# Output projections of a segment recurrence: rows stationary in four column tiles, weights moving, the last eight rows of four segments in one more pass

## The chip, the cores and the metric

One core of one Trainium2 chip runs the whole program. The metric is the device time of one execution in microseconds (us). Each kernel was run several times, in rounds that alternate with runs of the kernel before on the same chip. Most executions of one kernel agree within about 0.3%. Where stages are compared, each number is read from one profiled execution; profiles of two kernels can come from different chips of the same machine, so a stage difference of under about 15 us in the forward or backward stage is not used alone.

In the views PE is TensorE (PEld its weight loads), DVE VectorE, ACT ScalarE, POOL GpSimd and SP SyncE; L201 is a line of the kernel, x24 a count. A pair is a weight load and its matmul. The granted clock is the share of TensorE's full clock that was granted; the DMA share is the mean busy share of the core's 16 DMA engines.

## The reference, cut to what matters

A layer normalisation, a recurrent attention block A and a gated MLP block B, forward, and the gradients of all inputs. Block A works through 64 segments of 32 rows. Eight memory rows go ahead of each segment, so a segment has L = 40 rows, and the first eight rows of its output are the memory of the next one:

```python
for s in range(n_seg):                                  # 64, one after the other
    h = concatenate([mem, x[:, s*32:(s+1)*32, :]])      # 40 rows of 512
    q, k, v = (einsum('btd,dhe->bhte', h, W) for W in (Wq, Wk, Wv))   # 32 heads of 128
    ...                                                 # masked softmax, o = p v
    o = einsum('bhte,hed->btd', o, Wo)                  # output projection: 40 x 4096 by 4096 x 512
    mem = o[:, :8, :]                                   # to the next segment
    outs.append(o[:, 8:, :])
```

The backward pass goes through the segments in reverse. It has three such projections per segment, of dV, dK and dQ, summed into one 40 x 512 result; its first eight rows go to the segment before. The change touches these four projections and what is done with their results.

## The kernel before

A helper layer orders the instructions: it takes the program in source order, estimates readiness, and fixes an order for each engine. The output projection keeps a 128 x 128 block of the weight stationary and moves the 40 rows of a segment (as columns); the result is transposed, 128 features by 4 x 40:

```python
def outproj(pi):                                  # forward; before
    heads = range(pi * PG * 3, min(H, (pi + 1) * PG * 3))
    for c in range(DC):                           # 4 blocks of 128 features
        for h in heads:                           # 32 heads in three calls
            g_, hl = h // 3, h % 3
            nc.tensor.matmul(at_ps[0][:, c, :], lhsT=Wo[:, h, c * 128:(c + 1) * 128],
                             rhs=OT[:, g_ * GW + hl * L:g_ * GW + (hl + 1) * L], ...)
...
nc.scalar.activation(hT_next[:, :, 0:M], at_ps[0][:, :, 0:M], AF.Copy)   # memory of the next segment
nc.vector.tensor_copy(aoT[:], at_ps[0][:, :, M:L])
nc.gpsimd.dma_start(self.AOT[s], aoT[:])          # 32 rows, transposed, for the middle stage
```

The backward one, `dht`, is the same three times. The middle stage (MLP, in tiles of 128 rows) needs the rows upright, so it transposes them:

```python
# middle stage, tile j; before (cut)
nc.gpsimd.tensor_copy(aoC[:]..., aoT[:])          # GpSimd reorders
for c in range(DC):
    nc.tensor.transpose(tp[:, c, :], st["aoC"][:, c * 128:(c + 1) * 128], self.ident[:])
nc.scalar.activation(a_rows[:], tp[...], AF.Copy)  # ScalarE evicts
nc.vector.tensor_tensor(t0[:], a_rows[:], ga_bc[:], op=ALU.mult)
nc.vector.tensor_tensor(x1[:], t0[:], st["x0"][:], op=ALU.add)
```

The last stage (weight gradients in 44 groups of up to three heads, one 2 MB load `xt` each, issued by SyncE and GpSimd in turn, plus 16 layernorm tiles spread between the groups) does the same with the row gradients: four loads, four transposes, a VectorE copy and a GpSimd cast per tile. Its two side matrices take their memory rows by two transposed loads, `mt`, and transposes.

The softmax here doesn't subtract the row's maximum and nothing guards it: scores larger than these inputs give would overflow.

## Time and profile before

Before: 4352.75 us, median of four runs (4343.44 to 4357.68). The stages are cut at the first projection, the last forward projection, the first and last product of the backward segments, and the end; the lengths are read from the view that sums busy time by windows.

| stage (us) | before, first profile | before, second profile |
|---|---|---|
| forward segments | 1378.7 | 1394.5 |
| middle (MLP) | 695.6 | 697.3 |
| backward segments | 1306.9 | 1317.3 |
| last (weight gradients) | 847.7 | 846.8 |
| span | 4315.0 | 4342.0 |

### The profile page before, as it was taken

What the parts mean: (1) busy time and instruction counts of PE and PEld (TensorE: products, weight loads), DVE (VectorE), ACT (ScalarE), POOL (GpSimd) and SP (SyncE); (2) the same over time, 40 slices, a digit from 0 to 9 for tenths busy, and PEclk for the clock granted to TensorE, in tenths of its full rate; (3) what the DMA queues carried; (4) which work ended last, traced back from release to release, by engine and by line L of the source; (5) the groups of instructions that cost most, each with busy time, mean ns of one, the idle gap of its engine ahead of it and who ended that gap; (6) DMA issues with size and microseconds to landing.
All of it is one profiled execution on the core that took longest, in us unless ns stands there. A gap on an engine that the chain in (4) does not pass through costs nothing. (4 is left out here: it accounts for less than half of the span.)

```text
span 4315.0 us, 189475 instructions
## 1 busy us (share of the span) xinstructions
PE 3762.5 (87%) x87970; PEld 3165.2 (73%) x87970; DVE 1964.5 (46%) x3832; ACT 1537.9 (36%) x2685; POOL 807.3 (19%) x1063
## 2 busy tenths in 40 slices
PE   2989999999999688887988989898899949999996
PEld 2888888888888644444588889898888836666653
DVE  3444444444444377761233433343343346566554
ACT  0333333333343344441222222222222236556553
POOL 2111111111111133321111111111111112222210
PEclk6999999999999899998999999999999969999998
DMA  6223322233222422227754455455455498777873
GB/s 223 95 95 106 101 101 101 101 103 105 100 103 101 157 99 99 97 80 245 210 192 153 154 162 174 154 169 164 156 156 173 142 176 164 161 163 160 163 154 111
DMA packets 597548, 606.56 MB, mean 141 GB/s; under 512 B 404026, under 2 KB 492362, under 8 KB 595092
## 3 DMA queue, kind: packets, MB, share of 16 engines
q1 hardware_dynamic: 526756, 316.52, 28.2%
q0 software_dynamic: 64272, 264.56, 18.4%
q8 instruction: 687, 11.26, 1.1%
q10 hardware_dynamic: 5728, 13.37, 0.9%
q14 instruction: 105, 0.86, 0.1%
HBM read 319.30 MB, written 275.02 MB: 138 GB/s over the span
## 5 line engine op out<-in xcount | busy, mean ns | idle before, releaser
L1217 PE MATMUL gps<-rows,hrows 128*128 128x384 bf16 (+1 forms) x2640 | 461.9, 322 | 3.8 <-ACT ot L61 2.5
L1217 PEld LDWEIGHTS <-hrows 128*128 128x128 bf16 x2640 | 252.8, 98 | 139.0 <-issue 5.7
L63 DVE COPY rows<-tpg 128x384 bf16<-128x384 bf16 (+1 forms) x616 | 195.8, 347 | 265.5 <-PE tpg L1210 161.0
L1080 DVE CAST dh1T<-dh_ps 128x128 bf16<-128x128 f32 x64 | 18.7, 292 | 588.9 <-ACT dyT L1069 588.9
L1034 PE MATMUL dh_ps<-dQT,WqT 128*128 128x40 bf16 x8192 | 234.6, 182 | 55.1 <-issue 54.8
L347 PE MATMUL proj_ps<-hT,Wq 128*128 128x40 bf16 x8192 | 240.2, 180 | 34.0 <-issue 17.5
L1034 PEld LDWEIGHTS <-WqT 128*128 128x128 bf16 x8192 | 223.1, 98 | 61.1 <-issue 60.9
L1034 PE MATMUL dh_ps<-dKT,WkT 128*128 128x40 bf16 x8192 | 233.1, 179 | 37.8 <-issue 37.3
L347 PE MATMUL proj_ps<-hT,Wk 128*128 128x40 bf16 x8192 | 241.3, 180 | 22.7 <-issue 22.2
L347 PEld LDWEIGHTS <-Wq 128*128 128x128 bf16 x8192 | 229.1, 96 | 42.0 <-issue 41.5
L984 PE MATMUL proj_ps<-dyT,WoT 128*128 128x40 bf16 x8192 | 233.4, 181 | 23.0 <-ACT dyT L1069 18.0
L1034 PEld LDWEIGHTS <-WkT 128*128 128x128 bf16 x8192 | 222.1, 96 | 41.8 <-issue 41.3
L984 PEld LDWEIGHTS <-WoT 128*128 128x128 bf16 x8192 | 227.9, 97 | 30.2 <-issue 29.8
L1034 PE MATMUL dh_ps<-dVT,WvT 128*128 128x40 bf16 x8192 | 239.9, 179 | 9.0 <-issue 8.8
L347 PEld LDWEIGHTS <-Wk 128*128 128x128 bf16 x8192 | 227.0, 96 | 25.2 <-issue 25.1
L1203 ACT ACTIVATE xr<-xt 128x3072 bf16<-128x3072 bf16 (+1 forms) x44 | 235.3, 5349 | 11.2 <-DMA dhT<-DH1T 6.1
L347 PE MATMUL proj_ps<-hT,Wv 128*128 128x40 bf16 x8192 | 236.1, 180 | 2.7 <-issue 2.2
L1210 PEld LDWEIGHTS <-xr 128*128 128x128 bf16 x2560 | 180.3, 98 | 77.8 <-issue 28.4
L1034 PEld LDWEIGHTS <-WvT 128*128 128x128 bf16 x8192 | 227.3, 96 | 11.4 <-issue 11.2
L1210 PE MATMUL tpg<-ident,xr 128*128 128x128 bf16 x2560 | 218.1, 220 | 17.5 <-DVE rows L63 5.9
L347 PEld LDWEIGHTS <-Wv 128*128 128x128 bf16 x8192 | 226.4, 96 | 4.1 <-issue 3.9
L429 PE MATMUL at_ps<-OT,Wo 128*128 128x40 bf16 x8192 | 226.0, 179 | 0.0
(308 smaller groups left out, 7638.4 us busy)
## 6 DMA issues: line engine op xcount, KB each, us to landing
VT<-VT POOLq DMA_DIRECT2D x64, 384.0 KB, 2.7
OT<-OT POOLq DMA_DIRECT2D x64, 384.0 KB, 3.5
PS<-Pst POOLq DMA_DIRECT2D x64, 384.0 KB, 3.1
QST<-Qst POOLq DMA_DIRECT2D x64, 384.0 KB, 3.2
KST<-Kst POOLq DMA_DIRECT2D x64, 384.0 KB, 4.7
OT_l<-OT SPq DMA_DIRECT2D x64, 384.0 KB
VT_l<-VT SPq DMA_DIRECT2D x64, 384.0 KB
Pst_l<-PS SPq DMA_DIRECT2D x64, 384.0 KB
```

Source lines behind the costliest of these rows:

```text
L63: return nc.vector.tensor_copy(out, in_)
L347: nc.tensor.matmul(ps[:, g_, hl * L:(hl + 1) * L], lhsT=Ws[w][:, c, h * E:(h + 1) * E], rhs=hT[:, c, :], start=(c == 0), stop=(c == DC - 1))
L429: nc.tensor.matmul(at_ps[0][:, c, :], lhsT=Wo[:, h, c * 128:(c + 1) * 128], rhs=OT[:, g_ * GW + hl * L:g_ * GW + (hl + 1) * L], start=(n_a ...
L984: nc.tensor.matmul(ps[:, g_, hl * L:(hl + 1) * L], lhsT=WoT[:, c, h * E:(h + 1) * E], rhs=dyT[:, c, :], start=(c == 0), stop=(c == DC - 1))
L1034: nc.tensor.matmul(dh_ps[0][:, c, :], lhsT=WT[:, h, c * 128:(c + 1) * 128], rhs=X[:, g_ * GW + hl * L:g_ * GW + (hl + 1) * L], start=(n_dh ...
L1080: nc.vector.tensor_copy(dh1T[:], dh_ps[0][:, :, M:L])
L1203: nc.scalar.activation(xr[:, 0:cut, :], xt[:, :, 0:cut].rearrange("p s x -> p x s"), AF.Copy)
L1210: nc.tensor.transpose(ps[0:KR, hl, :], xr[:, c0:c0 + 2, :].rearrange("p a s -> p (a s)"), self.ident[:, :])
L1217: nc.tensor.matmul(ps[:, 0:nh * E], lhsT=hrows[0:KR, tp_, c * 128:(c + 1) * 128], rhs=rows[0:KR, tp_, 0:nh * E], start=(tp_ == 0), stop=(t ...
```

## The change

The intent: with 32 of the rows stationary and 128 weight columns moving, a product uses 32 of the 128 columns of the array, so four products for the four feature blocks run side by side. The eight rows that don't fit are collected for four segments (again 32 rows) and sent in one more pass. Results come out upright, as rows; only the memory rows need a transpose.

```diff
+    def col_mms(self, ps, lhsT, w, start, stop):
+        for c in range(self.cfg.DC):
+            self.nc.tensor.matmul(ps[32 * c:32 * c + 32, :], lhsT=lhsT, rhs=w[:, c * 128:(c + 1) * 128],
+                                  start=start, stop=stop, tile_position=(0, 32 * c))
...
-                    for c in range(DC):
-                        for h in heads:   # Wo stationary, 40 columns move
+                    for h in range(pi * PG * 3, min(H, (pi + 1) * PG * 3)):
+                        off = (h // 3) * GW + (h % 3) * L
+                        self.col_mms(at_ps[0], OT[:, off:off + 32], Wo[:, h, :], n_at[0] == 0, n_at[0] == H - 1)
...
-                    nc.scalar.activation(hT_next[:, :, 0:M], at_ps[0][:, :, 0:M], AF.Copy)
+                at_sb = sb2.tile([128, 128], BF16, name="at_sb")
+                nc.scalar.activation(at_sb[:], at_ps[0][:], AF.Copy)
+                tail.collect(s % nseg_t, [OT])          # GpSimd: rows 32..39 of this segment
+                tail.chunk()                            # a quarter of the pass of the last four segments
+                    self.rows_to_mem(psp, at_sb, hT_next)   # a transpose and a VectorE copy
+                tail.store_a(s, at_sb)
... (backward: the same for dV, dK, dQ)
... (middle stage)
-                nc.gpsimd.tensor_copy(aoC[:]..., aoT[:])
-                    nc.tensor.transpose(tp[:, c, :], st["aoC"][...], self.ident[:])   # x 4
-                nc.scalar.activation(a_rows[:], tp[...], AF.Copy)
+                self.load_x_rows(a_rows, j, self.AOA, self.AOB)      # eight loads per tile
... (last stage, per layernorm tile)
-                    nc.sync.dma_start(dhT[...], self.DH1T[j * nseg + s4])             # x 4
-                    nc.tensor.transpose(tp[:, c, :], dhT[:, c, :], self.ident[:])     # x 4
-                nc.vector.tensor_copy(dh[:], tp[...])
-                nc.gpsimd.tensor_copy(dhb[:], dh[:])
+                self.load_x_rows(dhb, j, self.DHA, self.DHB)         # eight loads per tile
... (side matrices: sixteen small loads of memory rows in place of two mt loads and eight groups of transposes)
```

## The prediction

> **What bounds the kernel now.** I first cut the span into its stages: forward segments (96 to 1470 us), middle (to 2150), backward segments (to 3475), weight gradients (to the end).
>
> ```profile
> core 0: us, PE busy (x) PEld busy (x) DVE busy (x) ACT busy (x) POOL busy (x), PEclk, DMA share, GB/s
> 96.00:1470.00 1374.00, 1250.37 (x39464) 1197.41 (x39463) 581.39 (x1202) 528.21 (x1158) 257.41 (x457) 0.99 0.30 101
> 2150.00:3475.00 1325.00, 1183.59 (x38180) 1155.76 (x38180) 502.82 (x1096) 310.89 (x641) 189.45 (x326) 0.97 0.51 161
> ```
>
> TensorE carries both segment stages, 21.5 and 20.7 us per segment (64 of each), with 617 and 597 matmuls per segment. The other engines are below half. The list of waits says what TensorE still waits for in the backward stage:
>
> ```profile
> PE dh_ps L1034 <- issue: 100.9, 105, 2.6
> PE proj_ps L984 <- ACT dyT L1069: 18.0, 63, 0.3
> ```
>
> "Issue" means that no operand was missing. The timeline of one such wait, beginning after 45 matmuls of a run of 128:
>
> ```profile
> 2709.64 2.17 PE L1034 MATMUL dh_ps<-dKT,WkT 128*128 128x40 bf16 x80
> 2711.65 1.28 PE L1034 MATMUL dh_ps<-dQT,WqT 128*128 128x40 bf16 x45
> 2714.82 2.26 PE L1034 MATMUL dh_ps<-dQT,WqT 128*128 128x40 bf16 x83 [1.89 <-issue]
> ```
>
> Counting matmuls from the end of that wait to the ends of the next ones:
>
> ```profile
> core 0: us, PE busy (x), PEclk, DMA share, GB/s
> 2714.80:2724.19 9.39, 8.26 (x256) 1.00 0.12 20
> 2724.20:2733.60 9.40, 7.93 (x256) 1.00 0.80 255
> 2733.60:2738.45 4.85, 4.22 (x128) 0.65 0.38 154
> 2738.45:2756.40 17.95, 15.90 (x512) 1.00 0.55 168
> ```
>
> All are multiples of 128. And the table of DMA queues has
>
> ```profile
> q8 instruction: 687, 11.26, 1.1%
> ```
>
> 687 packets of 16,384 bytes; 87,970 matmuls / 687 = 128. At 64 bytes an instruction (below), a packet is 256 instructions, 128 pairs of weight load and matmul. So TensorE's program arrives in blocks of 128 pairs, and TensorE stops where a block has not landed. I lined up the instruction packets with the block edges. Backward, a packet starts 1.05 us at the earliest (mean 1.7) after a block that had to be waited for begins, and TensorE goes on 2.2 to 2.6 us (mean 2.5) after that start. A packet started inside a block is thus the next block: only one is fetched ahead. My estimate of the time below which a block cannot go is therefore 1.7 + 2.5 = 4.2 us backward, where the data transfers take half of the DMA time; forward (0.30) about 3.7. Check: backward blocks that hold only projection matmuls last 4.3 us on average (41 blocks), although the same 128 matmuls run in 3.2 us when nothing stops them. The projections that this change speeds up are already bound by instruction delivery, not by the array.
>
> **What the Trainium skill says.** (1) "TensorE: Matmul & The Clock Gate", "Wait — 56ns, not 53.3ns?": start to start never falls below about 25 ns, however few columns move. The trace agrees: 80 matmuls of 40 columns in 2.17 us, less 0.18 for the last one's own length, is 25 ns. (2) Same page, "Part 3: Packing small matmuls", "Measured speedup vs the span model": tiles of one pack start some 4 ns apart and run together. The trace has a case, the 32-column matmuls over 384 columns in the prologue:
>
> ```profile
> 20.64 0.39 PE L190 MATMUL modrow_ps<-wmod,sclo_bc 128*32 128x384 bf16 x4
> 20.86 0.33 PE L190 MATMUL modrow_ps<-wmod,schi_bc 128*32 128x384 bf16 x4
> 21.02 0.33 PE L190 MATMUL modrow_ps<-wmod,sclo_bc 128*32 128x384 bf16 x4
> ```
>
> Four start every 0.16 us: what one alone needs for 384 columns. So column tiles do run together, and their weight loads hide. (3) "Trainium Architecture — The Big Picture", "The software stack": instructions have 64 bytes, and the streams are put into each engine's memory at load. The first agrees; the second does not, for the trace has the 687 packets during the run.
>
> **The change, part by part.**
> *Array time of the projections.* Each of the four projections (one in a forward segment, three in a backward one) was 128 pairs at 25 to 26 ns, 3.3 us. Now it is 32 heads x 4 column tiles, again 128 pairs. A group of four streams 128 columns, 53 ns plus a few (estimate: a third of the 0.16 us above): 32 x 56 ns = 1.8 us. Saved: 1.5 us forward, 4.6 backward per segment, if only the array counted.
> *Tail pass.* 128 more pairs per projection and four segments: 32 forward and 96 backward per segment, 0.45 and 1.35 us of array time. With the transpose of the memory rows the segments go to 650 and 694 matmuls. The built program has 96,124 matmuls, 8,154 more.
> *Chain from segment to segment.* Before: ACT copy of 32 columns (197 ns), TensorE idle 0.28 us. Now: ACT copy of 128 columns (estimate 0.3 us), a transpose (0.21 plus its load), a DVE copy (0.2), about 0.95 us with the handovers. The built order puts tail matmuls before the transpose in most segments, so the visible idle time is some 0.5 us, 0.2 more than before.
> *Array sum:* forward -1.5 + 0.45 + 0.2 = -0.8 us, backward -4.6 + 1.35 + 0.2 = -3.0 us per segment, together -245 us. This is the intended gain.
> *Delivery.* Backward goes from 597/128 = 4.66 blocks per segment to 694/128 = 5.42. Now a block takes 20.7/4.66 = 4.43 us. About one block per segment, the one with the dot products and the first 128-column matmuls, is bound by its own work (62 blocks of mean 4.85); the other 4.42 would all lie at the floor. With 4.1 us (4.2 less a little, as the same data is moved in more time): 4.42 x 4.1 + 4.85 = 23.0 us, +2.3 per segment, +147 us. With the floor at 3.4 it would be 19.9 us (-50); with 4.4, 24.3 (+230). Forward: unstalled segments take about 20.4 us, so 19.6 by array time. Blocks that start up to some 30 matmuls before the projection, or in its first hundred, are then shorter than 3.7 us and are stretched to it; averaged over all positions this gives back about 1 us, and late packets in the q, k, v projections (0.5 to 0.7 us per segment now) stay. 21.2 us against 21.4, and some 0.3 for more switches between tile shapes (the trace has 0.10 us at one, instead of 0.027): net about +10 us for the stage.
> *Middle stage.* 64 transposes, 16 ACT and 16 POOL copies go, 7 more loads per tile come on SP. TensorE waits there for other things (ACT duT 43 us, weights 24 us): -5.
> *Last stage.* TensorE waits 41 us for the reordered memory tiles, but the first xt lands only at 3519.9 us, which holds the start anyway. The two mt loads are 16,384 packets of 64 bytes (15 ns each over 16 engines: 15 us of saturated DMA); about 4,000 packets of 256 bytes replace them: -10. Per tile a DVE cast of 0.66 us and four transposes go, and DVE's layernorm work is in the last chain: -10. Sum -20.
> *POOL* gains the collecting copies, some 1 to 2 us per segment, off the path.
> Total: 4351 + 147 + 10 - 5 - 20 = 4483; I lean slightly to the lower side, as some packets will find quieter DMA: 4475 us.
>
> **Rivals.**
> *The array sets the pace* and delivery follows: 4351 - 245 - 25 = about 4080 us. For it: 87% busy TensorE, concurrent tiles shown. Against it: stops exactly at block edges, and pure projection blocks at 4.3 us instead of 3.2.
> *Delivery binds at its best value* (3.3 to 3.4 us per block everywhere): backward -50 to -80, forward -40, rest -25: about 4210. For it: the smallest spacing of two packets is 3.25 us. Against: the mean under DMA load is 4.2.
> *The tiles do not run together* with 128 columns, each pair still taking 25 ns: the tail pass then costs 0.8 and 2.4 us per segment also in array time. Backward hidden behind delivery; forward +60 us: about 4540. Against: the 0.16 us groups.
> *The clock falls*, since TensorE would stand idle for half of each block: one stalled window above was granted 0.65. At half clock a block of column tiles takes 3.4 us, still under the floor, but the 128-column matmuls and the dot products slow: up to 100 us more, towards 4580.
> *A bank fewer for the rotating PSUM tiles* makes TensorE wait for evictions: DVE and ACT are below half busy; a few tens of us at most.
>
> **Range and chances.** Block floors of 3.7 to 4.4 us backward (about +30 to +230), forward -50 to +60, rest -25: 4340 to 4590 for 8 times in 10. Faster by over 2% (below 4264) needs nearly the best delivery everywhere or a wrong theory: 0.09. Within 2%: 0.25. Slower by over 2% (above 4438): 0.66.
>
> **What would show it.** Right: TensorE's idle time on "issue" in the backward stage grows from some 100 to 400 us or more, its busy time falls; groups of four start about 56 ns apart between stops; about 751 instruction packets; the backward stage lasts some 1470 us, the forward one 1360 to 1400; waits fall at multiples of 128 matmuls. Wrong: a backward stage under 1300 us, blocks of column tiles below 3.3 us, or two blocks fetched ahead (the array rival); groups at 100 ns (no concurrency); a granted clock near 0.7 there (the clock rival).

## The result, and the profile after

After: 4402.91 us, median of four runs (4396.22 to 4405.3), against 4352.75: slower by 1.15%, ratio 1.0115 with a 95% interval of 1.0094 to 1.0136. The interval leaves out 1, so the loss is clear of the noise, small as it is. The forecast was +124 us and the measurement is +50.

The stages, from the view by windows; columns as in the prediction (window, length, busy time of each engine, granted clock, DMA share, GB/s). After:

```profile
86.70:1432.30 1345.60, 1243.03 (x41839) 1147.52 (x41839) 585.90 (x1235) 531.96 (x1166) 244.91 (x475) 1.00 0.30 104
1432.30:2065.70 633.40, 551.17 (x3802) 303.83 (x3790) 319.45 (x573) 230.57 (x365) 153.28 (x128) 0.95 0.50 157
2065.70:3536.00 1470.30, 1155.08 (x44351) 1034.57 (x44351) 490.79 (x1102) 315.37 (x640) 216.41 (x464) 0.92 0.44 144
3536.00:4403.50 867.50, 738.69 (x5886) 476.38 (x5874) 460.87 (x876) 447.36 (x490) 113.69 (x88) 0.94 0.72 154
```

The second profile of the kernel before:

```profile
86.10:1480.60 1394.50, 1262.07 (x39694) 1208.04 (x39692) 587.35 (x1216) 529.98 (x1160) 257.46 (x455) 0.98 0.30 100
1480.60:2177.90 697.30, 573.53 (x3866) 319.53 (x3889) 377.08 (x577) 244.19 (x386) 175.57 (x148) 0.92 0.45 144
2177.90:3495.20 1317.30, 1182.28 (x38143) 1159.83 (x38144) 500.50 (x1087) 310.27 (x639) 184.34 (x320) 0.96 0.51 160
3495.20:4342.00 846.80, 741.20 (x5957) 480.72 (x5977) 478.15 (x898) 450.86 (x495) 170.89 (x104) 0.94 0.76 158
```

Stage by stage, after less before: forward -49, middle -64, backward +153, last +21. (Against the first profile: -33, -62, +163, +20.) The backward stage holds more matmuls (44,351 against 38,143) but TensorE is busy for less of it, 1155 us against 1182, and the stage is longer.

Where TensorE stood in the backward stage after the change, from the list of waits (what waited, for what, us in all, times, longest), and the table of DMA queues:

```profile
PE dh_ps L201 <- issue: 233.2, 122, 4.5
PE dh_tps L201 <- issue: 46.8, 42, 2.0
PE proj_ps L1004 <- issue: 23.6, 28, 1.3
```

```profile
q8 instruction: 751, 12.30, 1.2%
```

"Issue", waiting for no operand, is now 304 us. All the stops on issue of this stage, counted in the trace, begin at the same count of matmuls modulo 128. 751 instruction packets for 96,124 matmuls are again 128 pairs a packet. One block of it, from the timeline of TensorE:

```profile
2602.50 0.52 PE L201 MATMUL dh_ps<-WkT,dKT 128*32 128x128 bf16 x24 [2.64 <-issue]
2602.84 1.62 PE L201 MATMUL dh_ps<-WqT,dQT 128*32 128x128 bf16 x104
2606.24 0.52 PE L201 MATMUL dh_ps<-WqT,dQT 128*32 128x128 bf16 x24 [1.77 <-issue]
```

The 24 and 104 matmuls are one block of 128. Their 26 later groups of four take 1.62 us less the last one's own 0.18, 55 ns a group, as predicted: the column tiles do run together. Then TensorE stands for 1.77 us. The block takes 3.74 us from start to start, and its matmuls fill less than 2 us of that.

### The profile page after: what moved, and what is told of

Read it like the earlier page. It is cut to its first block, busy times and chain, and to the rows that moved or that the text cites. A ratio compares the mean times of both kernels' runs of the same rounds, so it can differ in the third digit from the quotient of the medians.

```text
span 4403.5 us, 205821 instructions
## 1 busy us (share of the span) xinstructions
PE 3700.6 (84%) x96124; PEld 2971.5 (67%) x96124; DVE 1878.4 (43%) x3840; ACT 1528.5 (35%) x2666; POOL 748.9 (17%) x1191
## 5 line engine op out<-in xcount | busy, mean ns | idle before, releaser
L201 PE MATMUL dh_ps<-WqT,dQT 128*32 128x128 bf16 x8192 | 176.2, 252 | 148.1 <-issue 147.7
L1004 PE MATMUL proj_ps<-dyT,WoT 128*128 128x40 bf16 x8192 | 242.7, 183 | 26.8 <-issue 23.6
L201 PEld LDWEIGHTS <-dQT 128*32 128x32 bf16 x8192 | 154.6, 114 | 159.6 <-issue 159.3
L209 DVE COPY dyT<-memtp 128x32 bf16<-128x32 bf16 x63 | 10.9, 174 | 567.4 <-PE memtp L208 567.4
L201 PE MATMUL dh_ps<-WkT,dKT 128*32 128x128 bf16 x8192 | 154.0, 222 | 80.1 <-issue 79.8
L61 ACT ACTIVATE dOT<-proj_ps 128x480 bf16<-128x480 f32 (+2 forms) x192 | 68.4, 391 | 433.7 <-PE proj_ps L1004 424.0
L63 DVE CAST KT<-proj_ps 128x480 bf16<-128x480 f32 (+2 forms) x256 | 119.6, 488 | 211.1 <-PE proj_ps L371 206.2
L61 ACT ACTIVATE QT<-proj_ps 128x480 bf16<-128x480 f32 (+2 forms) x256 | 104.9, 436 | 279.7 <-PE proj_ps L371 277.6
L1219 DVE COPY xr<-xt 128x4608 bf16<-128x4608 bf16 (+1 forms) x44 | 176.3, 4008 | 48.7 <-DMA dhb<-DHA 48.7
```

The lines of the kernel that those rows point to most:

```text
L61: return nc.scalar.activation(out, in_, AF.Copy)
L63: return nc.vector.tensor_copy(out, in_)
L201: self.nc.tensor.matmul(ps[32 * c:32 * c + 32, :], lhsT=lhsT, rhs=w[:, c * 128:(c + 1) * 128], start=start, stop=stop, tile_position=(0, 3 ...
L209: nc.vector.tensor_copy(dst[:, :, 0:M], tp[:, :, 0:M])
L1004: nc.tensor.matmul(ps[:, g_, hl * L:(hl + 1) * L], lhsT=WoT[:, c, h * E:(h + 1) * E], rhs=dyT[:, c, :], start=(c == 0), stop=(c == DC - 1))
L1219: nc.vector.tensor_copy(xr[:, cut:W, :], xt[:, :, cut:W].rearrange("p s x -> p x s"))
```

## The experiments

First a control, a second profile of the kernel before.

> A second look at the kernel before, because its first profile (4315 us) lies 37 us under the median of its timed runs (4353 us), so that stage by stage the change looks like +88 us while the timed runs say +50. If the first profile was a lucky one, this one comes out near 4350 us with the 37 us spread over the two segment stages (later instruction packets). If the profiler itself makes the kernel before quicker, it is again near 4315. In both cases the middle stage, from the last forward projection to the first backward dot product, should be 695 us as in the first profile.

4344.07 us, one look. Its stages are the second column of the table above; the timed difference of 50 us fits this profile (+61) better than the first (+88).

### Backward: array or delivery?

**tail_none** takes the tail pass out of the backward stage but for four heads, so that there are as many pairs per segment as before the change, but in column tiles. The tail rows are wrong (the comparison with the reference did not notice: the affected part is small).

```diff
         order = [(i, h) for i in range(self.n) for h in range(H)]
+        if self.n > 1:
+            order = order[:4]
```

> The changed kernel with the backward tail pass cut to its first four heads (wrong result on purpose): 92 pairs fewer per segment, 1.29 us of array time by groups of 56 ns. Delivery theory: 602 pairs are 4.70 blocks of 128 pairs instead of 5.42; at 4.0 to 4.2 us a block the segment loses 2.9 to 3.0 us, the backward stage falls from 1470 to about 1280 to 1290 us and the whole to about 4215 to 4225 us (0.97 of before). Array theory: 64 x 1.29 = 83 us less, about 4320.

4266.88 us, ratio 0.9811 (0.9794 to 0.9828). The backward stage:

```profile
2060.10:3400.40 1340.30, 1064.34 (x38463) 953.68 (x38463) 492.69 (x1102) 315.06 (x639) 215.76 (x463) 0.89 0.48 158
```

The same number of pairs as before the change (38,463 against 38,143) with 118 us less busy time, and the stage is not shorter than before but 23 us longer. If the array set the pace, three projections at 1.8 us instead of 3.3 would have saved some 4.6 us per segment, 290 us. So the array does not set it. The total lies 45 us above what I expected from delivery alone; the granted clock is down to 0.89 and the mean block took 4.46 us, as before the change (4.4) and not as in the changed kernel (4.24).

**tail_n8** leaves the number of instructions as in the changed kernel and makes each tail product move 8 columns instead of 128.

```diff
+                        for c in range(cfg.DC):
+                            self.k.nc.tensor.matmul(st["ps"][32 * c:32 * c + 32, 0:8], lhsT=tiles[i][:, h, :],
+                                                    rhs=ws[i][:, h, c * 128:c * 128 + 8], start=False, ...)
```

> The changed kernel with the backward tail pass moving 8 columns instead of 128 in all but its first head (wrong result on purpose): the same number of instructions, but a sixteenth of the streaming. Delivery theory: the blocks hold as many pairs as before, so the backward stage stays at 1470 us and the whole at 4400 us, within 15 us. Array theory: a group takes perhaps 25 ns instead of 56, so 23 groups save 0.7 us per segment, 45 us or more in all: 4355 or less.

4434.06 us, ratio 1.022 (1.0196 to 1.0245): less work for the array, and slower than the changed kernel by 31 us.

```profile
2063.20:3563.50 1500.30, 1152.65 (x44351) 1050.49 (x44351) 496.50 (x1102) 315.36 (x640) 216.43 (x464) 0.83 0.43 141
```

The array theory (4355 or less) is refuted. The stage got 30 us longer at a granted clock of 0.83 instead of 0.92: that the two go together is seen, that the clock is the cause is not shown.

**half_loads** keeps the program as it is and lets every second segment of the backward stage reuse the data of its neighbour, so that half of the data loads go away. The result is wrong.

```diff
             def get_loads(s):
+                if s % 2 == 0 and s + 1 in loads:
+                    loads[s] = loads[s + 1]
                 if s not in loads:
```

> The changed kernel with the five 384 KB loads of a backward segment made only for every second segment (wrong result on purpose): about a third of the backward stage's DMA traffic goes, the instructions of TensorE stay. If the packets with the instructions come late because of that traffic (theory: forward, with 0.30 of the DMA time in use, a block goes down to 3.5 to 3.7 us; backward, with 0.5, to 4.1), the block falls by 0.2 to 0.4 us and the backward stage by 70 to 140 us, the whole to 4260 to 4330. If the time of a block is the same whatever the traffic, the whole stays at 4400.

4315.54 us, ratio 0.9942 (0.9927 to 0.9957).

```profile
2062.20:3445.60 1383.40, 1114.40 (x44350) 1000.38 (x44351) 490.93 (x1102) 315.35 (x640) 216.43 (x464) 0.95 0.32 108
```

TensorE's program is unchanged, its waits for loaded data are some 2 us in both, and still the stage is 87 us shorter: with a DMA share of 0.32 instead of 0.44 the blocks come faster (mean 3.99 us instead of 4.24). About half of the 87 us is less waiting on issue (261 us instead of 307, with the small rows of the list), the other half less busy time of the same matmuls (1114 us instead of 1155) at a higher granted clock; the runs don't separate the two.

Where the data slows the instructions can be counted in the traces, in the stretches of one block between two stops on issue. From the start of the next packet TensorE goes on for 2.4 to 2.5 us, in both profiles of the kernel before, in the changed kernel, in tail_none and in half_loads, and the packet itself takes 1.1 us in each. But it starts 2.2 us (2.4 in the second profile) after the block's beginning in the kernel before (DMA share 0.51) and in tail_none (0.48), 1.7 in the changed kernel (0.44) and 1.5 in half_loads (0.32). So the wait for the packet's start is longer where more data moves, which also fits tail_none's being slower than I expected.

**four_bwd** keeps the idea of four tiles but takes four heads in them instead of four feature blocks: each tile holds the rows of another head and moves all 512 weight columns. The four partial sums are added by a small product with a matrix of four stacked identities. The same arithmetic now takes 32 pairs per projection instead of 128. (Its first builds did not fit in the on-chip memory; a few buffers became single.)

```diff
+    def head_mms(self, ps, lhsTs, ws, start, stop):
+        for q in range(4):
+            self.nc.tensor.matmul(ps[32 * q:32 * q + 32, :], lhsT=lhsTs[q], rhs=ws[q],
+                                  start=start, stop=stop, tile_position=(0, 32 * q))
+    def parts_to_mem(self, psp, part_sb, dst):
+        for c in range(DC):   # adds the four parts and transposes them
+            nc.tensor.matmul(tp[:, c, :], lhsT=part_sb[:, c * 128:(c + 1) * 128], rhs=self.sum4[:, :], ...)
```

> Another form of the backward projections: the four column tiles hold four different heads, each moves all 512 columns of its weights, and four partial sums are added at the end by small products with a matrix of four identities. It needs a quarter of the pairs (96 instead of 384 per segment, 24 instead of 96 for the tail, 8 more for the sums), but the array streams as long as in the changed kernel (24 groups of four at 0.215 us = 5.2 us, tail 1.3). Delivery theory: 342 pairs are 2.7 blocks, delivery stops binding, and array time takes over: dot products 3.3, 128-column matmuls 4.7, projections 5.2, tail 1.3, sums and chain about 1.5, together 16 to 17 us per segment instead of 23: backward stage 1020 to 1100 us, the whole 3980 to 4040 us (0.92). Array theory (delivery never mattered): no gain from fewer instructions, 4400 or a little more for the sums.

3961.31 us, ratio 0.9127 (0.9113 to 0.914), correct. The backward stage, the longest wait in it, and the instruction queue:

```profile
2060.60:3109.60 1049.00, 1032.34 (x21813) 700.73 (x21817) 518.49 (x1181) 335.87 (x640) 216.28 (x464) 1.00 0.60 199
```

```profile
PE rowsp L205 <- DVE dh_tpt L1409: 11.8, 15, 0.8
```

```profile
q8 instruction: 575, 9.42, 1.0%
```

The stage falls from 1470 to 1049 us. "Issue" has left the list of waits; the granted clock is 1.00, although the DMA engines are busier than ever (0.60). A block now takes 6.1 us of TensorE's own work. This is the strongest evidence for delivery: same products, a quarter of the instructions in the projections (21,813 matmuls in the stage instead of 44,351), 421 us less than in the changed kernel and 268 less than before. The clock can't explain it: 1155 busy us at 1.00 instead of 0.92 would be some 90 us less (estimate from these two views). Nor can the 64 bytes by which the added constant moves the later tiles: pad_after, below, has them and a backward stage of 1465.6 us.

**four_both** does it in the forward stage too.

> The same form in the forward segments too (32 pairs instead of 128, tail 8 instead of 32, 8 more for the sums). Forward segments then hold 537 pairs, 4.2 blocks; the array streams as long as in the changed kernel. Delivery theory: the blocks around the projection are no longer stretched, but the chain from segment to segment has a copy of 512 instead of 128 columns: between 0 and 60 us less than the version with the backward form alone, 3930 to 4040 us. Array theory: equal to that version or up to 40 us slower for the longer chain.

3950.67 us, ratio 0.9106 (0.9091 to 0.9121), correct. The forward stage is 1328.6 us instead of the 1341.3 of four_bwd (the three later kernels with this form have 1326.2 to 1329.2): there delivery was a small part.

**bwd_old** is the changed kernel with the old backward projections and the old handling of their results in the last stage.

> The new form in the forward segments and the middle stage, the old form in the backward segments (and in what the last stage reads of them). Theory (the backward stage is bound by instruction delivery and pays for 25% more pairs, forward and middle stage win): backward stage back at about 1305 us, forward 33 and middle 62 us under before, last stage about as before or up to 20 us slower: 4255 to 4290 us, about 0.98 of before. Rival (the backward stage got longer for another reason, such as the bank of PSUM less or the longer chain): the same number, so this run does not test that rival; but if forward and middle stage do not keep their gain without the new backward form, it comes out near 4350.

4234.17 us, ratio 0.9741 (0.9725 to 0.9757), correct.

```profile
86.10:1427.40 1341.30, 1240.25 (x41838) 1146.24 (x41839) 585.67 (x1235) 532.06 (x1166) 244.37 (x474) 1.00 0.30 104
1427.40:2062.60 635.20, 549.27 (x3777) 303.71 (x3793) 318.89 (x573) 230.61 (x365) 154.74 (x130) 0.95 0.50 157
2062.60:3381.40 1318.80, 1181.75 (x38142) 1158.37 (x38143) 500.58 (x1087) 310.10 (x639) 183.68 (x319) 0.97 0.51 160
3381.40:4229.90 848.50, 739.03 (x5942) 478.79 (x5962) 475.38 (x895) 449.62 (x493) 170.84 (x104) 0.94 0.77 158
```

So the change is two changes: the forward half gains 115 us (4349.6, the kernel before in the same rounds, less 4234.17), the backward half loses 169 (4402.91 less 4234.17).

### Middle: why 64 us and not 5?

The list of waits has it, before and after the change:

```profile
PE tp L665 <- ACT duT L61: 43.4, 14, 4.3
```

```profile
PE tp L683 <- ACT duT L61: 4.4, 14, 0.3
```

A wait of about 3 us per tile for a copy on ScalarE is gone, though the change doesn't touch that copy. The timeline of a tile before the change shows the chain (start, length, engine, operation, and the idle time before it with its cause):

```profile
1717.86 0.39 PE L597 MATMUL tp<-ident,aoC 128*128 128x128 bf16 x4
...
1718.98 0.59 ACT L599 ACTIVATE a_rows<-tp 128x512 bf16<-128x512 bf16 x1
...
1720.14 1.09 DVE L604 TENSOR_TENSOR t<-a_rows,ga_bc 128x512 f32<-128x512 bf16 x1
1720.65 4.01 POOL L657 TENSOR_TENSOR umh<-u,hh 128x1792 bf16<-128x1792 bf16 x1
1721.32 3.89 DVE L606 TENSOR_TENSOR x<-t,x 128x512 f32<-128x512 f32 x1
...
1727.65 0.63 ACT L618 ACTIVATE xh<-xhf 128x512 bf16<-128x512 f32 x1 [7.59 <-DVE xhf L617]
...
1728.19 0.58 ACT L720 ACTIVATE dh2b<-mm 128x512 bf16<-128x512 f32 x1
...
1733.33 0.55 PE L665 MATMUL tp<-ident,dg 128*128 128x128 bf16 x7 [3.61 <-ACT duT L61]
```

The transposes stand late in TensorE's order, so the rows reach VectorE late; the sum `x` then runs beside GpSimd's `umh` and takes 3.89 us; `xh` waits for it; and in ScalarE's order `dh2b`, and everything after it down to `duT`, stands behind `xh`. "SBUF — State Buffer", section "Who interferes with whom", says that a VectorE instruction with two inputs in SBUF contends with a GpSimd instruction that reads SBUF; the trace agrees: of the 16 tiles in this profile, the 12 with `umh` beside the sum have it at 3.9 us, the four without GpSimd work beside it at 0.7. After the change the rows come by DMA:

```profile
1609.74 0.60 ACT L738 ACTIVATE dh2b<-mm 128x512 bf16<-128x512 f32 x1 [4.17 <-PE mm L734]
...
1614.77 0.55 PE L683 MATMUL tp<-ident,dg 128*128 128x128 bf16 x7 [0.31 <-ACT duT L61]
...
1620.88 0.68 DVE L624 TENSOR_TENSOR x<-t,x 128x512 f32<-128x512 f32 x1
```

Here `dh2b` follows its product at once, `x` takes 0.68 us, and the wait is 0.31 us.

**mid_detour** tests it: in the changed kernel the rows are loaded as after the change, but pass TensorE (four products with the identity) and a ScalarE copy, as before.

```diff
+                tpa = psT.tile([128, D], F32, name="tpa", tag="t")
+                for c in range(DC):
+                    nc.tensor.matmul(tpa[:, c * 128:(c + 1) * 128], lhsT=self.ident[:],
+                                     rhs=st["a_raw"][:, c * 128:(c + 1) * 128], start=True, stop=True)
+                nc.scalar.activation(a_rows[:], tpa[:], AF.Copy)
```

> The changed kernel, but in the middle stage the loaded attention rows go once more through TensorE (four products with the identity) and an ACT copy before they are used, as they did before. Theory: the 62 us that the middle stage won came from the chain aoC transposes, ACT copy, DVE sums, which put the ACT copy of xh in front of dh2b and duT in ACT's order, so TensorE waited 3.6 us per tile for duT. Then the middle stage goes back from 633 us to about 690 and the whole to about 4455 us (1.024 of before), with about 40 us of waits of the transposes of dg on ACT duT. Rival 1: it was the POOL copy aoC or the smaller DMA traffic, which stay away here; then the time stays at 4403 plus 5 us or less. Rival 2: the removed TensorE and ACT work itself (16 tiles of 0.9 us): +10 to +15 us.

4447.6 us, ratio 1.0229 (1.0211 to 1.0246). The middle stage and the wait:

```profile
1426.90:2115.20 688.30, 565.69 (x3836) 316.92 (x3852) 370.17 (x573) 241.64 (x381) 153.38 (x129) 0.93 0.46 145
```

```profile
PE tp L688 <- ACT duT L61: 39.4, 14, 3.9
```

688 us instead of 633, and the wait is back. The way through TensorE and ScalarE is what cost 55 of the 64 us, through its place in two engines' orders. That the 3.89 us of `x` is one link of it is read from the timeline, not tested by itself.

### Forward: what does the tail pass cost?

The forward stage lost 49 us where I had +10. **fwd_tail4** cuts the forward tail pass to four heads (wrong).

```diff
+        if self.n == 1:
+            order = order[:4]
```

> The changed kernel with the forward tail pass cut to its first four heads (16 of 128 pairs per four segments, so about 28 pairs fewer per segment; the tail rows of the output are wrong on purpose). It asks why the forward stage fell from 1394 us (second profile of the kernel before) to 1346 instead of rising by 10. If the tail pass fills idle slots of TensorE, cutting it saves little: forward stage 1330 to 1350, whole 4385 to 4405. If it costs its full array time of 0.45 us per segment, or a quarter of a delivered block (0.25 x 4.1 us = 1.0 us per segment), the stage falls by 25 (to 1320) or by 58 us (to 1287).

4375.35 us, ratio 1.007 (1.0047 to 1.0093). The forward stage is 1321.0 us, some 18 to 26 us below the twelve other kernels here that have this forward stage with its full tail pass (1339.4 to 1346.8). 1,790 matmuls fewer at 14 ns are 25 us. So the tail is paid at about its array time, the second of the three answers, and my idea that it only fills idle slots falls. The waits show how both are true in part. In the changed kernel:

```profile
PE or_ps L434 <- DVE Vst L428: 13.7, 33, 0.4
PE tps L383 <- DVE Ost L436: 10.4, 34, 0.3
```

With the tail cut:

```profile
PE or_ps L434 <- DVE Vst L428: 24.0, 63, 0.5
PE tps L383 <- DVE Ost L436: 19.9, 65, 0.3
```

Before the change:

```profile
PE or_ps L410 <- DVE Vst L404: 26.4, 64, 0.4
PE tps L359 <- DVE Ost L412: 20.0, 65, 0.3
```

The tail filled 20 us of these waits, but waits on issue and the longer busy time take that back.

### Last stage: four tries, and what stays open

The last stage got 20 us longer. Reading the trace group by group, the delay is 3 us at the first of the 44 groups, 16 us at the ninth and 20 at the end: most of it arises at the start, where the 2 MB loads are issued later. One stretch of it (columns as in the view by windows above), 60 to 100 us after the stage's start, before and after the change:

```profile
3527.30:3567.30 40.00, 35.63 (x274) 23.71 (x274) 28.86 (x60) 24.33 (x24) 17.54 (x12) 0.89 0.97 193
```

```profile
3596.00:3636.00 40.00, 31.81 (x247) 21.47 (x248) 26.75 (x55) 22.94 (x22) 9.36 (x8) 0.84 0.65 135
```

DMA share 0.65 instead of 0.97: the engines have less to do, because the next large load isn't issued. On GpSimd that load stands behind the layernorm tile's operations after the change, and ahead of them before it. Before:

```profile
3531.67 2.77 POOL L1199 DMA_DIRECT2D xt<-DQT  x1 [60.04 <-ACT rows L61]
3534.46 0.84 POOL L1121 TENSOR_TENSOR rstd<-ve,mhalf 128x1 f32<-128x1 f32 x1
```

After (73 us into the stage instead of 64):

```profile
3605.93 0.56 POOL L1135 TENSOR_TENSOR rstd<-ve,mhalf 128x1 f32<-128x1 f32 x1 [63.88 <-DVE ve L1133]
3608.18 1.16 POOL L1142 TENSOR_TENSOR pr<-dhb,xh 128x512 bf16<-128x512 bf16 x1 [1.68 <-DVE xh L1137]
3609.28 2.83 POOL L1214 DMA_DIRECT2D xt<-DQT  x1
```

I tried four single causes on the changed kernel. **rows_act** moves the eight small loads per tile to ScalarE's queue:

```diff
-                self.load_x_rows(dhb, j, self.DHA, self.DHB)
+                self.load_x_rows(dhb, j, self.DHA, self.DHB, nc.scalar)
```

> The changed kernel with the eight small loads of row gradients per layernorm tile of the last stage issued by ScalarE's queue instead of SyncE's, so that they don't stand ahead of the large loads in SyncE's order. If that queue is what costs the last stage 20 us: last stage about 850 instead of 867, whole about 4385. If the start of the stage (small pieces for the two side matrices) is it: last stage stays at 862 to 872, whole 4395 to 4410.

4402.93 us, ratio 1.013 (1.0114 to 1.0147), last stage 877.0. **late_dy** loads the second side matrix before the twelfth group:

```diff
-                dyrows = build_side_rows(self.DAROWS, "dyrows", mem_dy)
+                        if gi == 12:
+                            dyrows = build_side_rows(self.DAROWS, "dyrows", mem_dy)
```

> The changed kernel with the second side matrix (2 MB and ten small pieces, needed only for the last quarter of the weight gradients) loaded before the twelfth of the 44 groups instead of at the start of the last stage. If the start of the stage, where DMA is saturated, costs the 20 us: last stage 840 to 852. If SyncE's order of the small loads in the steady part is the cause: 862 to 872, as after the change.

4401.1 us, ratio 1.0126 (1.0107 to 1.0144), last stage 868.4. The first group starts 9 us earlier than in the changed kernel, and the gain is gone by the eighth. **rows_few** makes four loads of the eight (wrong):

```diff
+                for s4 in range(nseg):   # 32 rows each, the last 8 are not the right ones
+                    nc.sync.dma_start(dhb[s4 * T:(s4 + 1) * T, :]..., self.DHA[nseg * j + s4]...)
```

> The changed kernel, last stage: the row gradients of a layernorm tile come in four loads of 32 rows instead of four of 24 and four of 8 (the last 8 rows of a segment are memory rows instead, wrong on purpose). In the built program every load that SyncE issues first waits for the load eight issues earlier, as eight semaphores go round; 13 issues per tile instead of 9 would thus hold SyncE behind stores that haven't landed. If the number of small loads is the cause of the 20 us: last stage 848 to 855 instead of 867, whole about 4387. If not: 863 to 872.

4394.69 us, ratio 1.0108 (1.0079 to 1.0138), last stage 866.3. **last_detour** sends the loaded rows through TensorE, VectorE and GpSimd as before:

```diff
+                    nc.tensor.matmul(tp[:, c * 128:(c + 1) * 128], lhsT=self.ident[:],
+                                     rhs=raw[:, c * 128:(c + 1) * 128], start=True, stop=True)
+                nc.vector.tensor_copy(dh[:], tp[:])
+                nc.gpsimd.tensor_copy(dhb[:], dh[:])
```

> The changed kernel in which the rows of a layernorm tile of the last stage, loaded as after the change, pass through TensorE (four products with the identity), a VectorE copy and a GpSimd cast, as they did before the change; the values stay right. In the built programs of the changed kernel the layernorm tiles have run ahead: on GpSimd and SyncE more of their operations stand before each large load of transposed data than before the change; with the way through TensorE the orders look as before again. If that order costs the 20 us, the last stage is 845 to 853 us although work is added, and whole 4380 to 4388; if the pieces at the start or the small loads do, it stays at 865 to 872, whole 4400 to 4408.

4407.52 us, ratio 1.012 (1.01 to 1.014), last stage 874.8. All four causes fall, each taken alone. Of the kernels whose tiles lie at the same address (next section) only bwd_old, which undoes all of it (loads, their number, the way through TensorE, the second side matrix), has 848.5. What is shown: where most of the 20 us is lost, and that the new side matrix of the forward pass does not cost them. Which combination of the rest does stays open.

### The address of the last stage's tiles

In four_bwd the last stage, the same code as in the changed kernel, took 851 us instead of 867. Its 256-byte packets, nearly all of them SyncE's large loads, took 18.0 ns in the mean instead of 23.4. The added constant of 64 bytes per partition had moved all later tiles, in the built program from 448 bytes beyond a multiple of 512 to a multiple (the traces show no addresses). **pad_after** adds an unused constant of that size to the changed kernel, **pad_before** to the kernel before.

```diff
         make_identity(nc, self.ident[:])
+        pad = const.tile([128, 32], BF16, name="pad64")
+        nc.vector.memset(pad[:], 0.0)
```

> The changed kernel with an unused constant of 64 bytes per partition, which moves all later tiles by 64 bytes: the tiles of the last stage then start at multiples of 512 bytes of a partition (as in the kernels with four heads in four tiles) instead of 448 bytes beyond one. In those kernels the 256-byte packets of the last stage took 18.0 ns, in the changed kernel 23.3 ns, for the same loads. If the address decides that: 18 ns and a last stage of 845 to 855, whole about 4388. If it is something else in those kernels: 23 ns, 867 and 4400.

> The kernel before with the same unused 64 bytes. It shows whether the comparison of before and after is touched by the address: both stand at 448 bytes beyond a multiple of 512. Theory of the address: 256-byte packets of the last stage 18 ns instead of 23.4, last stage 825 to 840 instead of 847, whole 4325 to 4340. Rival: 23 ns and 4345.

pad_after: 4379.79 us, ratio 1.0075 (1.0045 to 1.0104), last stage 851.7. pad_before: 4346.6 us, ratio 0.999 (0.9954 to 1.0027), last stage 839.3. The table of DMA queues over the last stage (packets, MB, share of 16 engines), changed kernel:

```profile
q1 hardware_dynamic: 223356, 78.93, 44.4%
q0 software_dynamic: 12416, 48.27, 24.4%
```

With the 64 bytes:

```profile
q1 hardware_dynamic: 223356, 78.93, 36.6%
q0 software_dynamic: 12416, 48.27, 18.2%
```

Equal packets and bytes, and a fifth less DMA time; the 256-byte packets took 18 ns in both padded kernels. The address theory holds: 16 us of this stage after the change, 8 before it. "DMA: Bandwidth & Descriptors", section "How a descriptor splits into AXI transactions", says that when a transfer does not start at a multiple of 256 bytes, its first transaction starts at the multiple below and the bytes before the start still cost time. It says so of reading, and these loads write to the tiles that moved; the runs agree in direction, but don't tell 256 from 512. For the comparison of before and after it changes little, as both stand at the same bad address; but 16 us of what four_bwd gains (last stage 851 us instead of 867) is this, not instructions, and four_both lies at the good address too. In the whole time of pad_before the 8 us are not told from noise.

### Putting it together

**four_last** is four_both with the edits of rows_act and late_dy.

> The best version so far (four heads in four column tiles in both directions, 3951 us) with both edits of the last stage, small loads on ScalarE's queue and the second side matrix late. If the edits help as the two runs beside it say, 3915 to 3940 us; if neither is the cause, 3945 to 3955.

3935.4 us, median of four runs (3930.89 to 3942.32), ratio 0.9054 (0.9037 to 0.9071), correct, last stage 840.8. It is the fastest kernel, although neither edit helped the changed kernel alone. **four_row1** (rows stored in row order by GpSimd, in five stores per segment and sixteen per tail pass, one load per tile, second side matrix late) and **four_best** (the way through TensorE of last_detour, second side matrix late) were meant to beat it:

```diff
+            for c in range(4):                     # four_row1
+                self.k.nc.gpsimd.dma_start(self.k.DHR[32 * s:32 * s + 24, c * 128:(c + 1) * 128],
+                                           rows_sb[32 * c + 8:32 * c + 32, :])
-                self.load_x_rows(dhb, j, self.DHA, self.DHB)
+                nc.sync.dma_start(dhb[:], self.DHR[r0:r1, :])
```

> The best form (four heads in four column tiles in both directions) with the second side matrix loaded late and the row gradients stored in row order by GpSimd, so that a layernorm tile needs one load instead of eight. Theory of the many small loads: last stage 825 to 835 (840.8 in the version with the loads on ScalarE's queue), whole 3920 to 3930. Rival: 840 and 3935 or more; if the additional stores of GpSimd hurt the backward stage, it is above 1055 instead of 1050.

> The four-head form in both directions (3951 us; its last stage 857, at the good address) with that way through TensorE and the second side matrix loaded before the twelfth group. If the order theory is right: last stage 825 to 838, whole 3915 to 3932. If not: 840 to 857 and 3935 to 3952.

four_row1: 3976.09 us, ratio 0.9145 (0.912 to 0.917), last stage 881.1, backward stage 1049.7: both my expectation and the theory of many small loads fail; it is 13 us ahead of four_both at the first group and 24 us behind it at the 25th. four_best: 3949.97 us, ratio 0.9074 (0.9062 to 0.9087), last stage 849.9. The last stage reacts to how the layernorm tiles lie between the large loads by up to 40 us, and I can't predict which way.

## Why the prediction was right or wrong

The forecast was a sum of four stages, +132 us, lowered to +124. Measured were +50 timed and +61 between the two profiles (+153 - 49 - 64 + 21).

| term | predicted | measured (second profile of before; first) |
|---|---|---|
| backward stage | +147 | +153; +163 |
| forward stage | +10 | -49; -33 |
| middle stage | -5 | -64; -62 |
| last stage | -20 | +21; +20 |

**Backward, right.** Delivery sets the pace, one packet of 128 pairs at a time. The stage grew by 153 to 163 us where the prediction had 147, with 751 packets where it had 751, and groups at 55 ns where it had 56. That it came to 1470.3 us where the prediction had "some 1470 us" is partly luck, as the prediction cut the stage before the change 18 us longer (1325 us). Blocks that hold only projections, their tail and the transpose took 4.06 us in the mean (4.1 predicted), none below 3.47 (counted in the trace, from one block's first matmul to the next's). tail_none and tail_n8 refute the array, half_loads and four_bwd confirm delivery from two sides. The waits on issue came to 304 us, not "400 us or more". The clock rival may be real in part: 0.92 was granted here and 0.83 in tail_n8, but no run isolates it.

**Middle, the step that failed.** "TensorE waits there for other things (ACT duT 43 us, weights 24 us): -5." I read the wait for `duT` as unrelated because the change doesn't touch `duT`. It was the end of the chain that the change removes: the wait fell from 43 us to 4, and mid_detour brings it back to 39 us and the stage by 55. It is one of the two terms that were missed by 59 us.

**Forward, a mis-sized term.** The stage came near the array sum, "-0.8 us" per segment or -51 us (-33 to -49), and the tail's 0.45 us per segment in it is confirmed by fwd_tail4 (about 0.4). That the net agrees is partly luck: TensorE's busy time fell by only 13 us (19 against the second profile), and waits that the sum did not have went too, those for Vst and Ost from 46 us to 24, where the tail pass fills in. What failed is the give-back: "averaged over all positions this gives back about 1 us", and "some 0.3" for switches between tile shapes, which turned the -51 into +10. All waits on issue in the forward stage did not grow but fell, from 43 us (51 in the second profile) to 37; of these, those at the q, k, v projections, which were to "stay", fell from 41.8 to 27.0. I had put the floor of a forward block at 3.7 us and assumed that every short block would be stretched to it. In the trace the 42 blocks with at least 100 matmuls of the projection or its tail took 3.42 us in the mean, and only 20 of them ended in a stop on issue, 11.5 us in all.

**Last, wrong in sign.** "Sum -20" counted operations that go (an `mt` load of small packets, a cast, transposes). The start did not get faster (first group at 61 us instead of 58), and the loads in the first groups are issued later. +20, cause open, as told above.

**Rivals.** "The array sets the pace" (4080) and "delivery at its best value" (4210) fail on the backward stage; "the tiles do not run together" fails on 55 ns. Of a bank fewer, the waits of the backward stage show nothing: the longest that isn't issue is 3.1 us in all.

The errors, middle -59, forward -59, last +41, backward +6, add up to the -71 us from +132 to +61. The sign was right because the largest term was; the size was wrong because two gains of some 50 to 60 us were read as nearly nothing. The measured time lies inside the range of 4340 to 4590 us; the likeliest outcome by the prediction, slower by over 2% (0.66), did not come.

## What to carry to other kernels

Where TensorE waits for "issue" at a constant count of instructions, as here at every 128 pairs, count instructions and not array time: packing that kept the number of matmuls gained nothing here (tail_none), and packing that cut it to a quarter (512 moving columns, four heads side by side, one small product to add the parts) gained 421 us in one stage against the changed kernel, 268 against the one before. Before calling a wait unrelated to a change, follow it back through the in-order engines: the operation that ends it may stand behind one that the change moves. And when DMA is busy, check at which address the loaded tiles begin; 64 unused bytes were worth 16 us.

## What the Trainium skill lacked or had wrong

- "Trainium Architecture — The Big Picture", section "The software stack", has the instruction streams put into each engine's memory at load. "Runtime: NRT & Kernel Launch", section "Instruction fetch mechanics", which the prediction does not use, does have them streamed in blocks of 16 KiB, 256 instructions, as the runs show (687 packets of 16,384 bytes before, 751 after), but calls the cost of crossing a block mostly hidden. Here it was not: TensorE stood for 304 us at the ends of blocks in the backward stage after the change. Neither page says that a program of short matmuls is bound by this, nor that data transfers slow it (half_loads: 87 us).
- "TensorE: Matmul & The Clock Gate", Part 3, has the tiles of one pack running together, and the runs agree (55 ns a group of four), but says nothing on the delivery of the instructions that packing takes: with as many pairs as before, packed projections made the stage 23 us longer (tail_none), with a quarter of them 421 us shorter than in the changed kernel (four_bwd).
- "DMA: Bandwidth & Descriptors" tells how a read at an unaligned address splits, but gives no time for it, and no rule for where to place the tiles of a plain load in on-chip memory: 256-byte packets took 23.4 ns where the tiles began at 448 bytes beyond a multiple of 512 (by the built program) and 18.0 ns at a multiple.
